# Second channel matmul as seven products of half blocks in place of eight, in a fused attention and MLP-mixer kernel

## The chip, the cores and the metric

The kernel runs on one core of a Trainium2 chip. The metric is the device time of one execution in microseconds (us): the median of 16 runs, 273.47 us before the change (273.07 to 275.13). Five engines work side by side, each through its own queue in order: TensorE (PE, with its weight loads as PEld), VectorE (DVE), ScalarE (ACT), GpSimd (POOL) and SyncE (SP, which here only issues transfers). They wait for each other through semaphores.

## The reference

Eight batches of 576 positions, 8 heads of 64, f32 in and out.

```python
q_p = phi(q, cos_w, sin_w)          # relu(q)*cos | relu(q)*sin, 128 features a head
k_p = phi(k, cos_w, sin_w)
kv  = einsum('bhsf,bhsd->bhfd', k_p, v);  z = k_p.sum(axis=2)
x   = (q_p @ kv) / (q_p . z + 1e-6)           # [B, 576, 512]
u   = x + (relu(x^T @ w_tok1) @ w_tok2)^T     # token matmuls, 576 -> 256 -> 576
out = u + relu(u @ w_ch1) @ w_ch2             # channel matmuls, 512 -> 1536 -> 512
```

The change is in the last line: `relu(u @ w_ch1)` is called h1, and `h1 @ w_ch2` is the second channel matmul.

## The kernel before, in words

The 576 rows of a batch are spread over 128 partitions so that four full row tiles of 128 (J=4) and half a tile are left; the half tiles of two batches make one row tile. So each batch has a block of 4 x 128 rows, and the eight half tiles make a further block of 4 x 128 rows, the *tail* (`u_tail`, `uT_tail`). A block is what the channel matmuls work on.

All work is issued in an order written by hand. Batches 0 and 1 and the beginning of 2 and 3 come from the list `PLAN`. From batch 2 on, `channel(...)` issues a block's channel matmuls, and between them, at numbered *slots*, the work of the following batches that `hooks_for` has put there. While batch p's block is in `channel`, attention and token matmuls of batch n=p+1 are done, the features and transposes of m=p+2, and the loads of p+3.

`channel` (L576) has 12 steps for the first matmul (index mi): four matmuls of 512 columns into a PSUM tile `c_ps` from pool psM (four buffers), then a relu to `h1[:, mi, :]` in bf16 on ScalarE or VectorE, as `evac` says (L672), then the slot's hooks. The second matmul follows: for each of four row tiles j, 12 matmuls of 512 columns accumulate in `o_ps` (L606), VectorE adds the result to `u` (L609), and after the second and fourth row tile SP stores two of them. Each j has two slots (12 to 19). In the tail (`fine=True`) the last row tile is done in two column halves (L598, L600), and each row tile is stored at once by SP and ScalarE's queue (`store_tail`, L624).

Names that the prediction uses: `kvm`/`kvo` (L367, L377: kv of all heads: 40 narrow matmuls, and its copy on ScalarE), `numf`/`numfo` (L420, L425: q features times kv on TensorE, then two small VectorE instructions and a multiplication to `x`), `mix`/`mixo` (L429, L436: first token matmul and relu to `B1`), `um`/`uo`/`ubc`/`utx` (L456 to L474: second token matmul; VectorE adds `x` to give `u`; GpSimd casts to bf16 `ub`; a transposing transfer writes `uT`, the operand of the next block's first matmul), `tm`/`to`/`tb` (L485 to L503: the same for the half tile), `feat` (L323: a q or k feature, ScalarE "A" or VectorE "D"), `turnx` (L353: transposing transfer of q features to `qpT`), `cast` (L334: v to bf16 on GpSimd, "P"). Pools psA (two buffers of two banks) and psM are PSUM; `one` and `two` are pools with one and two buffers. A tile that is allocated again in a pool waits until the readers of the buffer's earlier tile are done.

`hooks_for` (L640) puts kv in slot 0, `num_all` in 2 to 6, `mix` in 7 and 8, `u_all` in 10, 11 and 12, the casts in 3 to 7, q features in 9 to 13 (two a slot, ScalarE), k features in 13 to 17 (two a slot, VectorE), `turnx` in 12, 15 and 16.

Of the kernel before, what the change touches and what calls it, by code (L numbers as in the profile page):

```python
# [9 lines left out]
F32 = mybir.dt.float32  # L10
BF16 = mybir.dt.bfloat16
AF = mybir.ActivationFunctionType
ALU = mybir.AluOpType

WARM = 20
FIRST = "S"
PLAN = """
feat.0.k.4.2.0.D feat.0.q.0.2.0.A feat.0.q.2.2.1.A feat.0.q.3.2.1.A feat.0.q.4.2.1.D feat.0.q.3.2.0.A
# [40 lines left out]
def kernel(  # L59
# [11 lines left out]
    nc = tc.nc  # L71

    B, H, S, D = q.shape
    Dm = H * D
    _, D_tok = moe_w_tok1.shape
    _, D_ch = moe_w_ch1.shape
    P = 128
    J = S // P
    JA = J + 1
    R = J + JA  # L80
    NP = B // 2
    NCC = Dm // P
    NT = D_tok // P
    NCH = D_ch // P
    HH = H // 2
    VW = D + 2
# [44 lines left out]
    def heads(g):  # L131
        return slice(0, H) if g == 2 else slice(g * HH, (g + 1) * HH)
# [30 lines left out]
    par = const.tile([P, 1], F32, name="par")  # L163
# [36 lines left out]
    for i in range(2):  # L200
        t = const.tile([P, JA, H, VW], BF16, name=f"vbf{i}")
# [7 lines left out]
    w2r = const.tile([P, NT, S], BF16, name="w2r")  # L209
    wc1 = const.tile([P, NCC, D_ch], BF16, name="wc1")  # L210
    wc2 = const.tile([P, NCH, Dm], BF16, name="wc2")
# [44 lines left out]
    u_tail = const.tile([P, NP, Dm], F32, name="u_tail")  # L256
    uT_tail = const.tile([P, NP, NCC, P], BF16, name="uT_tail")
# [8 lines left out]
    def relu(eng, dst, src):  # L266
        if eng == "A":
            nc.scalar.activation(dst, src, AF.Relu)  # L268
        else:
            nc.vector.tensor_relu(dst, src)  # L270

    class Batch:
# [4 lines left out]
        def sb(self, name):  # L277
            if not hasattr(self, name):
                pool, shape, dt = {
                    "kp": (one, [P, JA, H, 2, D], BF16), "qp": (one, [P, JA, H, 2, D], BF16),  # L280
                    "qpT": (two, [P, JA * H, P], BF16), "kv": (two, [P, H, VW], BF16),
                    "x": (two, [P, JA, Dm], BF16), "B1": (two, [P, NT, Dm], BF16),
                    "u": (two, [P, J, Dm], F32), "ub": (one, [P, J, Dm], BF16),
                    "uT": (two, [P, J, NCC, P], BF16), "h1": (one, [P, NCH, 4 * P], BF16)}[name]
                setattr(self, name, pool.tile(shape, dt, name=name))
            return getattr(self, name)
# [248 lines left out]
        def o(self, j):  # L535
            nc.vector.tensor_add(self.u[:, j, :], self.ps.pop(("o", j)), self.u[:, j, :])
            if j % 2:
                for p_ in range(2):
                    nc.sync.dma_start(out=out_rows(self.b, p_, j - 1, 2), in_=self.u[p_::2, j - 1:j + 1, :])
# [36 lines left out]
    def channel(uT, u, store, by_slot, hooks, fine=False):  # L576
        h1 = one.tile([P, NCH, 4 * P], BF16, name="h1")
        slot = 0

        def step():  # L580
            nonlocal slot
            for f in hooks.get(slot, ()):
                f()
            slot += 1

        for mi in range(NCH):
            c_ps = psM.tile([P, 512], F32, name="c_ps", tag="psM")
            for ki in range(NCC):
                nc.tensor.matmul(c_ps, wc1[:, ki, mi * P:(mi + 1) * P], uT[:, :, ki, :],  # L589
                                 start=(ki == 0), stop=(ki == NCC - 1))  # L590
            relu(by_slot[mi], h1[:, mi, :], c_ps)
            step()
        for j in range(4):
            if fine and j == 3:
                for cs in (slice(0, Dm // 2), slice(Dm // 2, Dm)):
                    o_ps = psM.tile([P, Dm // 2], F32, name="o_ps", tag="psM")
                    for ki in range(NCH):
                        nc.tensor.matmul(o_ps, h1[:, ki, j * P:(j + 1) * P], wc2[:, ki, cs],  # L598
                                         start=(ki == 0), stop=(ki == NCH - 1))
                    nc.vector.tensor_add(u[:, j, cs], o_ps, u[:, j, cs])  # L600
                    store(j, u, cs)
                break
            o_ps = psM.tile([P, Dm], F32, name="o_ps", tag="psM")
            for half in range(2):
                for ki in range(half * NCH // 2, (half + 1) * NCH // 2):
                    nc.tensor.matmul(o_ps, h1[:, ki, j * P:(j + 1) * P], wc2[:, ki, :],  # L606
                                     start=(ki == 0), stop=(ki == NCH - 1))
                if half:
                    nc.vector.tensor_add(u[:, j, :], o_ps, u[:, j, :])  # L609
                    store(j, u)  # L610
                step()

    def out_rows(b, par, j, n):
        f = JA * par + j if j < J else J
        return out[b].rearrange("(m r) c -> m r c", r=R)[:, f:f + n, :]

    def store_batch(b):
        def store(j, u):
            if j % 2:
                for par in range(2):  # L620
                    nc.sync.dma_start(out=out_rows(b, par, j - 1, 2), in_=u[par::2, j - 1:j + 1, :])
        return store

    def store_tail(j, u, cs=slice(0, Dm)):  # L624
        for c, eng in ((0, nc.sync), (1, nc.scalar)):
            eng.dma_start(out=out_rows(2 * j + c, c, J, 1)[:, :, cs], in_=u[c::2, j:j + 1, cs])


    bt = [Batch(b) for b in range(B)]
    OPS = {"ld": ld, "ldp": ldp, "mkid": lambda: make_identity(nc, ident), "wt1": wt1, "wt2": wt2, "wu": wu, "wd": wd, "w2a": w2a}  # L630
    keep_warm(WARM)
    for word in PLAN.split():
        name, *a = word.split(".")
        a = [int(x) if x.isdigit() else x for x in a]
# [5 lines left out]
    def hooks_for(n, m, nxt):  # L640

        h = {}

        def at(slot, f, *a):
            h.setdefault(slot, []).append(lambda: f(*a))
        if nxt is not None:
            at(0, load, nxt, "k")
            at(0, load, nxt, "q")
            if nxt > 5:
                at(9, load, nxt, "v")  # L650
        if n is not None:
            at(0, n.kv_all)
            for j in range(JA):
                at(2 + j, n.num_all, j)
            for j in range(JA):
                at(7 + j // 3, n.mix, j, 2)
            at(8, n.mix_out)
            for g in range(3):
                at(10 + g, n.u_all, g)
        if m is not None:  # L660
            for j in range(JA):
                at(3 + j, m.cast, j, 1, 2, "P")
                at(9 + j, m.q_feature, j)
                at(13 + j, m.k_feature, j)
            at(12, m.turnx, 0, 2)
            at(15, m.turnx, 2, 2)
            at(16, m.turnx, 4, 1)
        if nxt == 5:
            at(16, load, nxt, "v")
        return h  # L670

    evac = ["A"] * 7 + ["D", "A", "D", "D", "D"]  # L672
    for p in range(2, B):
        s = bt[p]
        n = bt[p + 1] if p + 1 < B else None
        m = bt[p + 2] if p + 2 < B else None
        nxt = p + 3 if p + 3 < B else None
        channel(s.uT, s.u, store_batch(p), evac if n else ["A", "D"] * 6, hooks_for(n, m, nxt))
    channel(uT_tail, u_tail, store_tail, ["A", "D"] * 6, {}, fine=True)

    _ = tile, bass_utils

# [29 lines left out]
```

## Time and profile before

| what | value |
|---|---|
| median of 16 runs | 273.47 us (273.07 to 275.13) |
| profiled execution | 273.31 us, its span 271.5 us |
| granted TensorE clock | 1.00 |
| batches 2 to 6 (start of the first channel matmul) | 88.1, 115.7, 143.3, 170.9, 198.4 us |
| batch 7, tail, last matmul ends | 226.0, 246.7, 267.5 us |
| VectorE busy in those five batches | 19.71, 18.88, 19.45, 17.58, 14.30 us |
| ScalarE busy in them | 12.51, 12.51, 12.51, 12.51, 6.39 us |
| GpSimd: cast of v, of ub (512, 1024 elements) | 0.614, 1.04 us |
| VectorE: k feature, numfo multiplication, relu from PSUM | 0.48, 0.69, 0.69 us |
| ScalarE: relu, q feature, relu to B1 | 0.60, 0.71, 1.02 us |
| landing of a transposing transfer, ub to uT, qp to qpT (median) | 3.2, 4.4 us |

The page gives for each engine its busy time and the number of its instructions; the stages give the same for a stretch of the span; the groups give one line of code on one engine, its shapes, count, total and mean time in ns, and then the idle time before it and what ended it. The chain of work is followed back from the last instruction to whatever released it, so it names what set the end. A matmul's duration in the groups (0.38 us for 512 columns) is longer than the distance from one to the next, since they overlap; the chain shows the distance.

### The profile page before, as it was taken

Reading aid. Unit: us, or ns where it says so; the run is one execution under the profiler, and the core shown is the slowest. Engines: PE = TensorE matmul, PEld = TensorE weight load, DVE = VectorE, ACT = ScalarE, POOL = GpSimd, SP = SyncE. Lnnn points to the kernel's source line nnn. Section 1 sums busy time; section 2 is a strip of 40 time slices with the busy share of each in tenths; the row PEclk is TensorE's granted clock in tenths of the full one; section 3 lists DMA queues with packets and bytes.
Section 4 is the critical chain, followed back from the end, with each engine's and each line's share of the span. In section 5 each row is a group of like instructions: output and inputs, shape, how many; then the busy total and the mean of one; then the engine's idle time right before and its main releaser. Section 6 shows DMA issues by size and latency. Waiting matters only on the chain.

```text
span 271.5 us, 4868 instructions
## 1 busy us (share of the span) xinstructions
PE 262.8 (97%) x1941; PEld 137.8 (51%) x1941; DVE 172.3 (63%) x346; ACT 111.1 (41%) x176; POOL 47.1 (17%) x67
## 2 busy tenths in 40 slices
PE   6988999999999999999999999999999999999994
PEld 2875556455444644464445544554455444444443
DVE  6489788899872658845794679467837643423422
ACT  2885281475490548044904490439033102201300
POOL 2154070040051043003350036003000210000000
PEclk9999999999999999999999999999999999999999
DMA  6999999999999999999999978900970062012012
GB/s 197 359 232 154 277 248 227 367 226 230 377 233 210 333 380 295 230 164 338 360 203 255 327 223 193 226 0 19 218 193 2 1 172 80 0 57 98 2 69 86
DMA packets 79079, 53.37 MB, mean 197 GB/s; under 512 B 47824, under 2 KB 76496, under 8 KB 79056
## 3 DMA queue, kind: packets, MB, share of 16 engines
q1 hardware_dynamic: 74512, 48.77, 66.8%
q0 software_dynamic: 4144, 3.77, 9.0%
q10 hardware_dynamic: 400, 0.52, 0.5%
q8 instruction: 15, 0.25, 0.3%
q14 instruction: 8, 0.07, 0.1%
HBM read 35.85 MB, written 9.44 MB: 167 GB/s over the span
## 4 chain that ended last, share of the span: by engine, by line
PE 91%; DVE 4%; DMA 3%; issue 0%; DVEq 0%
PE c_ps L589 27%; PE o_ps L606 26%; PE o L524 8%; PE c L512 8%; PE b L433 6%; PE u L460 5%; PE kv L361 4%; PE nf L390 3%; DMA kt<-in_k_dram 3%; PE ut L488 1%; PE tr L345 1%; DVE kp L332 1%; PE o_ps L598 1%; PE nm L390 1%; PE uT L450 1%; DVE x L413 1%
## 5 line engine op out<-in xcount | busy, mean ns | idle before, releaser
L268 ACT ACTIVATE h<-c_ps 128x512 bf16<-128x512 f32 x52 | 31.0, 597 | 107.6 <-PE c_ps L589 64.2
L606 PE MATMUL o_ps<-wc,h 128*128 128x512 bf16 x324 | 71.9, 379 | 0.0
L589 PE MATMUL c_ps<-uT,wc 128*128 128x512 bf16 x288 | 70.4, 379 | 0.0
L606 PEld LDWEIGHTS <-h 128*128 128x128 bf16 x324 | 31.7, 98 | 38.2
L589 PEld LDWEIGHTS <-wc 128*128 128x128 bf16 x336 | 30.8, 98 | 32.6
L270 DVE TENSOR_SCALAR h<-c_ps 128x512 bf16<-128x512 f32 x32 | 22.0, 688 | 28.4 <-PE c_ps L589 28.4
L264 POOL CAST ub<-u 128x1024 bf16<-128x1024 f32 x14 | 15.1, 1080 | 89.3 <-DVE u L465 45.8
L264 POOL CAST vbf<-vt 128x512 bf16<-128x512 f32 (+3 forms) x28 | 18.8, 708 | 64.9 <-DMA vt<-in_v_dram 51.5
L330 ACT ACTIVATE qp<-qt,cos_t 128x512 bf16<-128x512 f32 x33 | 23.1, 712 | 13.6 <-DMA qt<-in_q_dram 12.8
L609 DVE TENSOR_TENSOR u<-o_ps,u 128x512 f32<-128x512 f32 x24 | 16.6, 690 | 18.8 <-PE o_ps L606 18.6
L512 PE MATMUL c<-uT,wc 128*128 128x512 bf16 x96 | 22.7, 379 | 0.0
L524 PE MATMUL o<-wc,h 128*128 128x512 bf16 x96 | 22.0, 379 | 0.0
L413 DVE TENSOR_TENSOR x<-nf,den 128x512 bf16<-128x512 f32 x30 | 20.7, 691 | 1.0
L330 ACT ACTIVATE qp<-qt,sin_t 128x512 bf16<-128x512 f32 x30 | 21.1, 712 | 0.0
L465 DVE TENSOR_TENSOR u<-u,x 128x1024 f32<-128x1024 f32 x16 | 19.3, 1219 | 2.2 <-PE u L460 2.2
L332 DVE TENSOR_SCALAR kp<-kt,cos_t 128x512 bf16<-128x512 f32 x30 | 17.4, 584 | 4.9 <-DMA kt<-in_k_dram 4.9
L433 PE MATMUL b<-x,w 128*128 128x512 bf16 (+1 forms) x90 | 20.3, 355 | 0.0
L390 PEld LDWEIGHTS <-qpT 128*128 128x128 bf16 x320 | 15.3, 98 | 9.6 <-DVE x L413 1.5
L332 DVE TENSOR_SCALAR kp<-kt,sin_t 128x512 bf16<-128x512 f32 x31 | 17.5, 571 | 0.8 <-DMA kt<-in_k_dram 0.8
L460 PE MATMUL u<-B,w 128*128 128x512 bf16 x64 | 16.1, 379 | 0.0
L409 DVE TENSOR_SCALAR den<-nf 128x8 f32<-128x8 f32 x30 | 5.0, 166 | 15.9 <-PE nf L390 15.9
L524 PEld LDWEIGHTS <-h 128*128 128x128 bf16 x96 | 9.0, 97 | 10.2
(92 smaller groups left out, 250.4 us busy)
## 6 DMA issues: line engine op xcount, KB each, us to landing
out_dram<-u SPq DMA_DIRECT2D x32, 256.0 KB, 2.8
qt<-in_q_dram SPq DMA_DIRECT2D x8, 640.0 KB, 8.1
kt<-in_k_dram SPq DMA_DIRECT2D x8, 640.0 KB, 8.1
qt<-in_q_dram SPq DMA_DIRECT2D x8, 512.0 KB, 7.0
kt<-in_k_dram SPq DMA_DIRECT2D x8, 512.0 KB, 7.0
vt<-in_v_dram SPq DMA_DIRECT2D x6, 640.0 KB, 8.2
vt<-in_v_dram SPq DMA_DIRECT2D x6, 512.0 KB, 7.2
wc<-in_moe_w_ch_dram POOLq DMA_DIRECT2D x4, 384.0 KB, 7.7
```

The costliest lines, as they stand in the source:

```text
L264: (nc.scalar.copy if eng == "A" else ENG[eng].tensor_copy)(dst, src)
L268: nc.scalar.activation(dst, src, AF.Relu)
L330: nc.scalar.activation(dst, src, AF.Relu, scale=tab)
L332: ENG[eng].tensor_scalar(dst, src, scalar1=tab, scalar2=0.0, op0=ALU.mult, op1=ALU.max)
L390: nc.tensor.matmul(nm[:, hh * (D + 1):(hh + 1) * (D + 1)], self.qpT[:, j * H + h, :], self.kv[:, h, :D + 1], start=(not eps or hh == 0), s ...
L413: nc.vector.tensor_mul(dst, nmv[:, :, :, :D], den_b)
L433: nc.tensor.matmul(b1[:, mi], w1[:, col(self.c, j), mi * P:(mi + 1) * P], self.x[:, j, cs], start=(j == 0 and (g == 2 or mi == 0)), stop=( ...
L460: nc.tensor.matmul(ps[:, jj], w2[:, ki, 1 + 2 * g + jj, :], self.B1[:, ki, :], start=(ki == 0), stop=(ki == NT - 1))
L512: nc.tensor.matmul(ps, wc1[:, ki, mi * P:(mi + 1) * P], self.uT[:, :, ki, :], start=(ki == 0), stop=(ki == NCC - 1))
L524: nc.tensor.matmul(self.ps["o", j], self.h1[:, ki, j * P:(j + 1) * P], wc2[:, ki, :], start=(ki == 0), stop=(ki == NCH - 1))
L589: nc.tensor.matmul(c_ps, wc1[:, ki, mi * P:(mi + 1) * P], uT[:, :, ki, :], start=(ki == 0), stop=(ki == NCC - 1))
L606: nc.tensor.matmul(o_ps, h1[:, ki, j * P:(j + 1) * P], wc2[:, ki, :], start=(ki == 0), stop=(ki == NCH - 1))
```

## The change

The second matmul of a block is h1 (rows x 1536) times w_ch2 (1536 x 512). Both are cut into 2 x 2 quarters: h1 into a11, a12 (first two row tiles; contraction chunks 0 to 5 and 6 to 11), a21, a22 (last two), w_ch2 into q00, q01, q10, q11. Eight products of quarters are replaced by seven, with sums of quarters as operands and sums of products as results (a Winograd form of Strassen's scheme). For batches 2 to 7 (p from QUADS=2) and the tail, `channel7` takes the place of `channel`. Sums of the weights (`t1` in the place of q01, `t2`, `t3`, `t4`) are made once, in batch 2's slots 0 and 8. A product has 2 row tiles x 6 chunks = 12 matmuls with 256 columns. The sums of h1 (`s1`, `s2`, `a21` in place) are made by VectorE in bf16; the sums of products by VectorE, and GpSimd for two on `u22`, after ScalarE has copied three products from PSUM to f32 in SBUF (`va`, `vb`, `vc`). Slots 12 to 18 follow the products, and all stores of a block stand behind the last. Other moves: in these batches q features go to slots 1 to 6 and 9 to 12, k features to 7, 8 and 13 to 17, of which six of ten go to ScalarE; two relus go from VectorE to ScalarE (`evac7`); `u_all(2)` goes to slot 18; `qpT` and `x` have one buffer instead of two.

```diff
-                    "qpT": (two, [P, JA * H, P], BF16), "kv": (two, [P, H, VW], BF16),
-                    "x": (two, [P, JA, Dm], BF16), "B1": (two, [P, NT, Dm], BF16),
+                    "qpT": (one, [P, JA * H, P], BF16), "kv": (two, [P, H, VW], BF16),
+                    "x": (one, [P, JA, Dm], BF16), "B1": (two, [P, NT, Dm], BF16),
...
+    t1 = quad(0, 1)
+    def quad_weights():
+        return [lambda: nc.vector.tensor_sub(t3, quad(1, 1), quad(0, 1)),
+                lambda: nc.vector.tensor_sub(t1, quad(0, 1), quad(0, 0)),
+                lambda: nc.gpsimd.tensor_sub(t2, quad(1, 1), t1),
+                lambda: nc.vector.tensor_sub(t4, quad(1, 0), t2)]
...
+        a11, a12, a21, a22 = tok(0, 0), tok(1, 0), tok(0, 1), tok(1, 1)
...
+        for mi in range(NCH):
...
+            relu(by_slot[mi], h1[:, mi, :], c_ps)
+            if mi == NCH - 2:
+                s_part(s1, nc.vector.tensor_add, a21, a22, 0)
+                s_part(s2, nc.vector.tensor_sub, s1, a11, 0)
+            if mi == NCH - 1:
+                s_part(s1, nc.vector.tensor_add, a21, a22, 1)
+                s_part(s2, nc.vector.tensor_sub, s1, a11, 1)
+            step()
+        Dk = bank()
...
+            A = bank()
+            product(A, a11, quad(0, 0), True)
+            nc.scalar.copy(va, A)
+        nc.vector.tensor_sub(a21, a11, a21)
+        step()
+        product(Dk, a22, t4, True)
+        nc.scalar.copy(vb, Dk)
+        nc.gpsimd.tensor_sub(u22, u22, vb)
+        step()
+        Bk = bank()
+        product(Bk, s2, t2, True)
+        nc.vector.tensor_add(va, Bk, va)
+        nc.vector.tensor_sub(s2, a12, s2)
+        step()
+        C = bank()
+        product(C, s1, t1, True)
+        nc.scalar.copy(vc, C)
+        nc.vector.tensor_add(u12, u12, va)
+        nc.gpsimd.tensor_add(u22, u22, vc)
+        step()
+        product(Dk, a21, t3, False)
+        nc.vector.tensor_add(vb, Dk, va)
+        step()
...
+        product(C, s2, quad(1, 1), False)
+        if fine:
+            nc.vector.tensor_add(u2, u2, wide)
+            store(2, u, 2)
+            nc.vector.tensor_add(u12, C, u12)
+            store(0, u, 2, slice(D2, Dm))
+            step()
+            for jj in range(2):
+                product(A, a12, quad(1, 0), False, (jj,))
+                nc.vector.tensor_add(u11[:, jj], A[jj], u11[:, jj])
+            store(0, u, 2, slice(0, D2))
+        else:
+            nc.vector.tensor_add(u12, C, u12)
+            step()
+            product(A, a12, quad(1, 0), False)
+            nc.vector.tensor_add(u11, A, u11)
+            store(0, u, 2)
+            nc.vector.tensor_add(u2, u2, wide)
+            store(2, u, 2)
...
+            for i, slot in enumerate((1, 2, 3, 4, 5, 6, 9, 10, 11, 12)):
+                at(slot, m.feat, "q", i // 2, 2, i % 2, "A")
+            for i, slot in enumerate((7, 7, 8, 8, 13, 14, 15, 16, 17, 17)):
+                at(slot, m.feat, "k", i // 2, 2, i % 2, "D" if i < 4 else "A")
...
+    evac7 = ["A"] * 7 + ["D", "A", "A", "D", "A"]
+    evac2 = ["A"] * 4 + ["D", "A"] * 4
```

`s_part(..., n)` does chunks 0 to 3 (n=0) or 4 and 5 (n=1) of a quarter; `wide` reads `vb` twice, for both column halves; A, Dk, Bk and C are psM tiles, two of which take a second product later. In the prediction the products are counted in the order issued: A, D (the tile Dk), B, C, and then again into D, C and A.

More of the change, by code (lines that the diff above doesn't have):

```diff
@@ L15 @@
 WARM = 20
+QUADS = 2
 FIRST = "S"
@@ L611, in channel, with quad @@
                 step()
+    K2, D2 = NCH // 2, Dm // 2
+    t2, t3, t4 = (const.tile([P, K2, D2], BF16, name=f"t{i}") for i in (2, 3, 4))
+    def quad(a, b):
+        return wc2[:, a * K2:(a + 1) * K2, b * D2:(b + 1) * D2]
+    t1 = quad(0, 1)
[4 more added lines that the diff above has]
+                lambda: nc.vector.tensor_sub(t4, quad(1, 0), t2)]
@@ new lines, in channel7, with step, tok, s_part @@
+    def channel7(uT, u, store, by_slot, hooks, fine=False):
+        h1 = one.tile([P, NCH, 4 * P], BF16, name="h1")
+        slot = 0
+        def step():
+            nonlocal slot
+            for f in hooks.get(slot, ()):
+                f()
+            slot += 1
+        def tok(a, b):
+            return h1[:, a * K2:(a + 1) * K2, b * 2 * P:(b + 1) * 2 * P]
+        a11, a12, a21, a22 = tok(0, 0), tok(1, 0), tok(0, 1), tok(1, 1)
+        s1 = one.tile([P, K2, 2 * P], BF16, name="s1")
+        s2 = one.tile([P, K2, 2 * P], BF16, name="s2")
+        va = w2r.rearrange("p n s -> p (n s)").bitcast(F32)[:, :2 * D2].rearrange("p (a b) -> p a b", a=2)
+        vb = one.tile([P, 2, D2], F32, name="vb")
+        vc = one.tile([P, 2, D2], F32, name="vc")
+        u11, u12 = u[:, 0:2, :D2], u[:, 0:2, D2:]
+        u21, u22 = u[:, 2:4, :D2], u[:, 2:4, D2:]
+        def s_part(dst, f, a, b, n):
+            ks = (slice(0, 4), slice(4, K2))[n]
+            f(dst[:, ks], a[:, ks], b[:, ks])
+        def product(ps, a, b, first, jjs=(0, 1)):
+            for jj in jjs:
+                for ki in range(K2):
+                    nc.tensor.matmul(ps[jj] if isinstance(ps, list) else ps[:, jj], a[:, ki, jj * P:(jj + 1) * P], b[:, ki],
+                                     start=(first and ki == 0 and (jj == 0 or isinstance(ps, list))), stop=ki == K2 - 1,
+                                     skip_group_check=True)
+        def bank():
+            return psM.tile([P, 2, D2], F32, name="m_ps", tag="psM")
+        for mi in range(NCH):
+            c_ps = psM.tile([P, 512], F32, name="c_ps", tag="psM")
+            for ki in range(NCC):
+                nc.tensor.matmul(c_ps, wc1[:, ki, mi * P:(mi + 1) * P], uT[:, :, ki, :],
+                                 start=(ki == 0), stop=(ki == NCC - 1))
+            relu(by_slot[mi], h1[:, mi, :], c_ps)
[8 more added lines that the diff above has]
+        if fine:
+            A = [bank()[:, 0], psA.tile([P, D2], F32, name="m2_ps", tag="psA")]
+            for jj in range(2):
+                product(A, a11, quad(0, 0), True, (jj,))
+                nc.scalar.copy(va[:, jj], A[jj])
+        else:
[22 more added lines that the diff above has]
+        step()
+        wide = bass.AP(tensor=vb.tensor, offset=vb.offset, ap=[vb.ap[0], [D2, 2], [0, 2], [1, D2]])
+        u2 = u[:, 2:4, :].rearrange("p j (a d) -> p j a d", a=2)
+        product(C, s2, quad(1, 1), False)
+        if fine:
+            nc.vector.tensor_add(u2, u2, wide)
[3 more added lines that the diff above has]
+            step()
+            for jj in range(2):
+                product(A, a12, quad(1, 0), False, (jj,))
+                nc.vector.tensor_add(u11[:, jj], A[jj], u11[:, jj])
+            store(0, u, 2, slice(0, D2))
+        else:
+            nc.vector.tensor_add(u12, C, u12)
[5 more added lines that the diff above has]
+            store(2, u, 2)
+        step()
+        step()
@@ L617, in store_batch, with store, store_tail @@
     def store_batch(b):
[L618 to L621, printed above, removed]
-        return store
-    def store_tail(j, u, cs=slice(0, Dm)):
+        def store(j, u, n=1, cs=None):
+            if n == 1 and j % 2 == 0:
+                return
+            j -= j % 2
+            for par in range(2):
+                nc.sync.dma_start(out=out_rows(b, par, j, 2), in_=u[par::2, j:j + 2, :])
+        return store
+    def store_tail(j, u, n=1, cs=slice(0, Dm)):
+        rows = out.rearrange("b (m r) c -> m r b c", r=R)[:, J]
         for c, eng in ((0, nc.sync), (1, nc.scalar)):
-            eng.dma_start(out=out_rows(2 * j + c, c, J, 1)[:, :, cs], in_=u[c::2, j:j + 1, cs])
+            eng.dma_start(out=rows[:, 2 * j + c:2 * (j + n):2, cs], in_=u[c::2, j:j + n, cs])
     bt = [Batch(b) for b in range(B)]
@@ L670, in hooks_for, with hooks7, at @@
         return h
+    def hooks7(n, m, nxt, quads):
+        h = {}
+        def at(slot, f, *a):
+            h.setdefault(slot, []).append(lambda: f(*a))
+        if nxt is not None:
+            at(0, load, nxt, "k")
+            at(0, load, nxt, "q")
+            at(16 if nxt == 5 else 9, load, nxt, "v")
+        if n is not None:
+            at(0, n.kv_all)
+            for j in range(JA):
+                at(2 + j, n.num_all, j)
+            for j in range(JA):
+                at(7 + j // 3, n.mix, j, 2)
+            at(8, n.mix_out)
+            at(10, n.u_all, 0)
+            at(11, n.u_all, 1)
+            at(18, n.u_all, 2)
+        if m is not None:
+            for j in range(JA):
+                at(3 + j, m.cast, j, 1, 2, "P")
+            for i, slot in enumerate((1, 2, 3, 4, 5, 6, 9, 10, 11, 12)):
+                at(slot, m.feat, "q", i // 2, 2, i % 2, "A")
+            for i, slot in enumerate((7, 7, 8, 8, 13, 14, 15, 16, 17, 17)):
+                at(slot, m.feat, "k", i // 2, 2, i % 2, "D" if i < 4 else "A")
+            at(12, m.turnx, 0, 2)
+            at(14, m.turnx, 2, 2)
+            at(15, m.turnx, 4, 1)
+        if quads:
+            for f, slot in zip(quad_weights(), (0, 0, 0, 8)):
+                at(slot, f)
+        return h
     evac = ["A"] * 7 + ["D", "A", "D", "D", "D"]
+    evac7 = ["A"] * 7 + ["D", "A", "A", "D", "A"]
+    evac2 = ["A"] * 4 + ["D", "A"] * 4
     for p in range(2, B):
@@ L677 @@
         nxt = p + 3 if p + 3 < B else None
-        channel(s.uT, s.u, store_batch(p), evac if n else ["A", "D"] * 6, hooks_for(n, m, nxt))
-    channel(uT_tail, u_tail, store_tail, ["A", "D"] * 6, {}, fine=True)
+        if p < QUADS:
+            channel(s.uT, s.u, store_batch(p), evac, hooks_for(n, m, nxt))
+        else:
+            channel7(s.uT, s.u, store_batch(p), evac7 if n else evac2, hooks7(n, m, nxt, p == QUADS))
+    channel7(uT_tail, u_tail, store_tail, evac2, {}, fine=True)
     _ = tile, bass_utils
```

## The prediction

> **What bounds the kernel now.** I read the busy totals first, then the busy time by stage, then the chain that ended last in order of time. Totals (page, part 1), and two of the stages, one batch each (us, then PE, PEld, DVE, ACT, POOL busy, each with its count):
>
> ```profile
> PE 262.8 (97%) x1941; PEld 137.8 (51%) x1941; DVE 172.3 (63%) x346; ACT 111.1 (41%) x176; POOL 47.1 (17%) x67
> ...
> 115.70:143.30 27.60, 27.60 (x197) 13.88 (x196) 18.88 (x37) 12.51 (x20) 8.62 (x12) 1.00 1.11 270
> 226.00:246.70 20.70, 20.70 (x98) 9.41 (x96) 6.91 (x10) 3.58 (x6) 0.00 (x0) 1.00 0.13 51
> ```
>
> In a batch's 27.6 us TensorE is busy for 27.6, at a granted clock of 1.00, while the next engine, VectorE, has about 8 us free. So work taken from TensorE comes off the time, as long as no other engine becomes late. The chain of work, batch 3 and the end:
>
> ```profile
> 131.60 0.86 PE u L460 x4
> 132.47 1.29 PE o_ps L606 x6
> 133.76 0.43 PE ut L488 x2
> 134.19 9.06 PE o_ps L606 x42
> 143.26 0.86 PE c_ps L589 x4
> ...
> 257.09 7.77 PE o_ps L606 x36
> 264.86 2.63 PE o_ps L598 x24
> 267.52 0.42 DVE u_tail L600
> ```
>
> From 88 to 267.5 us the chain is TensorE alone. It gives both prices: a 512-column matmul takes 7.77/36 = 0.216, a 256-column one 2.63/24 = 0.1096, its own 98 ns weight load hidden.
>
> **What leaves and enters TensorE.** One second matmul is 48 x 0.216 = 10.36 (1.29 + 9.06). It becomes seven products of 12 matmuls with 256 columns: 84 x 0.1096 = 9.21, or 1.315 a product. Saved: 1.15 in each of batches 2 to 7 (the blocks from p=2 on), 6.9 in all. The tail costs 7.77 + 2.63 = 10.40 now: 1.19 saved. Together **8.1 us**. First matmul, attention and token matmuls are the same.
>
> A rule of the Trainium skill speaks against this: "TensorE: Matmul & The Clock Gate", section Back-to-back issue gap, gives sustained streams of weight load and matmul 131 ns at N=512 and 81 at N=128. By that, 48 matmuls are 6.3 us and 84 of width 256 (by a straight line between, an estimate, 98 ns) 8.2: the change would lose 1.9 a time. Here 512 columns take 216 ns and 256 take 110, so I use the rows.
>
> **What VectorE gets.** Per batch it loses six k features (6 x 0.48) and two relus (2 x 0.69), and four 0.69 adds are replaced. It gains four 512-element f32 adds (0.69: `va`, `vb`, and u12 twice), the u11 add (0.69), the wide u2 add (1.22, as L465), and bf16 adds within SBUF: `s1`, `s2` (1024 and 512 elements each), `a21` and the second `s2` (1536). The trace has no such add. Fast bound: 0.52 ns an element, as the bf16 copies at L264 (1024 in 682 ns, 512 in 417), so 0.42 / 0.68 / 0.95. Slow bound: 1.03 ns an element, as the f32 adds:
>
> ```profile
> L497 DVE TENSOR_TENSOR u_tail<-u_tail,x 128x512 f32<-128x512 f32 x4 | 2.8, 692 | 0.1
> ...
> L465 DVE TENSOR_TENSOR u<-u,x 128x1024 f32<-128x1024 f32 x16 | 19.3, 1219 | 2.2 <-PE u L460 2.2
> ```
>
> that is 0.69 / 1.22 / 1.75. All operands are bf16 with unit step; "VectorE: DVE Perf Modes", The perf-mode tier table, gives tensor_tensor twice its f32 rate in that case; no row here shows it. I take the fast bound. The six ops then cost 4.1 us (slow: 7.3).
>
> Whether they hide is decided in queue order. Let t=0 be the end of first-matmul tile 10. TensorE then does um(0), tile 11, um(1) (0.86 each), A and D: the third product, which needs `s2`, can start at 2.6 + 2.6 = 5.2. VectorE's queue: relu 0.69, s1 0.68, s2 0.68, uo(0) 1.22, s1 0.42, s2 0.42: 4.1, so 1.1 spare. Then uo(1) 1.22 and a21 0.95: 6.3, needed by the fifth product at 7.85. `va` waits for the third product (6.5), then 0.69, then s2 0.95: 8.2, needed by the sixth at 9.2: 1.0 spare. No stall. `u11`, `u2` and the tail-row add run into the next batch's first 2.2 us or so; its first VectorE work (numfo) is due after about 4.1.
>
> **ScalarE.** Sixteen features (11.4), ten relus (6.0), kv and B (1.6), three PSUM copies (1.8 by the relu's 0.6): 20.8 of some 26.4 us. Tight only in slots 1 to 6, where q features now stand: relu + feature 1.31 against TensorE's 0.86 + 0.26 = 1.12, so it falls 1.1 behind; the four psM buffers allow about three tiles, 3.4. From slot 7 it has over 2 us with one tile. The first q feature also waits until the transposes of the preceding q features (now one `qpT` buffer, one `qp`) have landed: the last is issued some 0.5 us into the batch, lands in 4.4 (part 6), near 5; the relus behind it would hold TensorE only past 6 to 6.5. The vb copy is due at 7.85 and ready near 5.9. No charge.
>
> **GpSimd and the queues.** Two f32 adds a batch. Nearest row: a one-input 512-element cast, 0.61; two inputs by "GPSIMD Engine Reference", Elementwise — side-by-side cycle accounting, take about twice VectorE's time, an estimate of 1.4; I take 1.4, due only at u2's add. The same page, Key points, warns of shared SBUF interfaces when VectorE has two SBUF inputs. This trace shows sharing between casts and k features:
>
> ```profile
> 138.72 0.48 DVE L332 TENSOR_SCALAR kp<-kt,cos_t 128x512 bf16<-128x512 f32 x1
> 139.12 0.83 DVE L332 TENSOR_SCALAR kp<-kt,sin_t 128x512 bf16<-128x512 f32 x1
> ...
> 138.78 3.70 POOL L264 CAST vbf<-vt 128x512 bf16<-128x512 f32 x5 [3.94 <-DMA vt<-in_v_dram]
> ```
>
> 0.48 becomes 0.83, and five casts take 3.70 instead of 2.84. Now ub's casts meet the second s1/s2 pair and a21, and the first u22 add the last s2: +0.35 each, two on the third product's path (spare 1.1), one on the sixth's (spare 1.0). Still covered; without the warning these spares stand whole.
>
> SP issues as many transfers per batch; turnx of q moves ahead of the stores, stores behind the seventh product. What gets closer is `uT`: uo(1), ubc (1.04), utx (landing 3.2) end at 5.3 to 5.7 + 1.1 + 3.3 = 10; the next batch needs it after 5.2 + 5 x 1.315 + 0.43 = 12.2. Only in batch 3 a v load is in flight, and a landing took 6.3: 0 to 1.1 late. I charge 0.3. The weight differences (three 1536-element VectorE subtractions, one on GpSimd, once) lie at batch 2's start, where VectorE is idle some 3 us.
>
> **End.** Now the last add ends 0.45 after TensorE. Then the wide add (waiting for GpSimd near 7.3 after the first matmul's end) 1.22, u12 0.69, u11 twice 0.42 end about 0.65 after: +0.2. All four tail rows are stored within 1.3 us instead of one every 2.6, and the last store has 128 KB per queue (2.0 to 2.3 us to landing now) not 64 (1.8 to 2.1): +0.2, and 0 to 0.8 for queueing: I take 0.3. End: +0.7.
>
> **Sum.** The profiled execution took 273.31 (span 271.5 plus 1.8), 0.16 under the median 273.47. 273.31 - 8.1 + 0.7 + 0.3 = 266.2; with a part of the 0.16, **266.3**.
>
> **Rivals.** (1) *Cover holds*, above: 265.2 to 267.6 (the end at 0.4 to 1.5, the uT wait at 0 to 1.1, the matmul at 0.1085 to 0.1096). 62%.
> (2) *Partly late*: port sharing or ScalarE's lag uses up spares of about 1 us, each of the five full batches stalls 0.3 to 0.8: 266.3 + 1.5 to 4 = 267.8 to 270.3. For: the spares are shorter than two or three +0.35. Against: they need overlap at the worst places. 23%.
> (3) *Slower: VectorE's queue becomes the bound between tile 10 and the sixth product.* At the slow bound its durations add to 5.7 at the third product's operand (due 5.2), 8.7 at a21, and 8.7 + 0.69 + 1.75 = 11.2 at the last s2, due at 9.2: 2.0 per full batch, 10 in five: 275.9. Overlapped starts (the trace has about 0.09 between an instruction's start and its forerunner's end) would make it 1.2, 272; GpSimd sharing adds back. It decides from 7.4/5 = 1.5 us a batch. For: no row shows the fast rate. Against: the bf16 copies do run at the fast rate, and VectorE's total stays under the period. 9%.
> (4) *Narrow matmuls don't keep 110 ns*: with weight loads binding at 123, seven products cost what eight did: 273.3 to 274, with the end. Against: 24 in a row at L598 and the 256-column ones at L433. 6%.
>
> The range 265.2 to 269.6 takes (1) and most of (2). A measurement tells apart about 0.2%, 0.55 us: faster 0.87, same 0.03, slower 0.10.
>
> **What will show it.** Right: product matmuls 12 in 1.31, TensorE without gaps in batches, period 26.4 against 27.6, the 1536-element VectorE adds near 0.95. Wrong: these at 1.75; idle TensorE time ahead of the third, fifth or sixth product put to VectorE; ahead of a batch's first matmul put to the uT transfer; c_ps waiting for a relu on ScalarE in slots 5 to 7; the last store over 1.5 us later after TensorE's end.

## The result, and the profile after

The changed kernel takes 269.42 us (median of 8 runs, 268.59 to 270.35) against 273.56 before (45 runs): a ratio of 0.9848, 95% interval 0.9836 to 0.9861. It is faster by 4.1 us; the forecast said 7. The time lies only 0.2 us inside the upper end of the range (269.6); a ninth execution of 271.96 us is on record and isn't among these eight, and with it the median would be 269.66, just outside. The profiled execution took 270.35 us, 0.9 above the median, its span 268.2.

First the totals (page, part 1) and the two stages, batch 3 and batch 7 (us, then PE, PEld, DVE, ACT, POOL busy):

```profile
PE 256.0 (95%) x2181; PEld 161.2 (60%) x2181; DVE 200.8 (75%) x367; ACT 143.5 (53%) x236; POOL 76.5 (29%) x82
```

```profile
114.74:141.99 27.25, 26.55 (x233) 17.29 (x231) 22.41 (x39) 18.36 (x31) 11.51 (x13) 1.00 1.04 281
223.23:242.76 19.53, 19.53 (x133) 12.93 (x132) 11.94 (x18) 6.53 (x11) 3.14 (x3) 1.00 0.17 61
```

Batch 7, with no other work between its matmuls, went from 20.70 to 19.53: the 1.2 us that were promised. Batch 3 went only from 27.60 to 27.25, and for the first time TensorE isn't busy all through it. Batches 2 to 6 take 26.58, 27.25, 27.44, 27.40 and 26.40 (they were 27.6 each), the tail from its start to its last matmul 19.5 instead of 20.8. The chain of work says what the gaps of batches 3 and 4 are:

```profile
116.88 0.88 PE c_ps L667 x4
...
117.78 0.18 ACT h L269
117.96 3.13 DMA qpT<-qp
...
121.33 0.72 ACT qp L331
122.05 0.49 ACT h L269
...
135.38 1.68 POOL ub L265
137.06 0.03 POOL u L691
137.09 4.76 DMA uT<-ub
...
141.99 1.02 PE c_ps L667 x4
...
159.83 9.17 PE m_ps L657 x84
```

The last of these lines is the price of seven products, 9.17 us, or 0.1092 a matmul. The others are two waits: a q feature (L331) on ScalarE that waits for a transposing transfer, with the relu (L269) that TensorE needs standing behind it; and batch 4's first matmul that waits for `uT`. The same wait of ScalarE stands at 145.75 in batch 4 and 171.49 in batch 5.

The new VectorE and GpSimd work (groups, shapes kept apart; the last columns are busy us, mean ns):

```profile
L701 DVE TENSOR_TENSOR u<-u,w2r 128x512 f32<-128x512 f32 x6 | 9.5, 1575 | 0.0
L702 POOL TENSOR_TENSOR u<-u,vc 128x512 f32<-128x512 f32 x6 | 9.3, 1548 | 1.9 <-ACT vc L700 1.5
...
L687 DVE TENSOR_TENSOR h<-h 128x1536 bf16<-128x1536 bf16 x7 | 6.6, 945 | 0.0
L652 DVE TENSOR_TENSOR s<-s,h 128x512 bf16<-128x512 bf16 x7 | 6.6, 936 | 0.2
...
L652 DVE TENSOR_TENSOR s<-h 128x1024 bf16<-128x1024 bf16 x7 | 4.8, 681 | 0.0
...
L652 DVE TENSOR_TENSOR s<-h 128x512 bf16<-128x512 bf16 x7 | 2.9, 416 | 0.0
```

1536 elements take 945 ns, 1024 take 681 and 512 take 416: the forecast's fast bound. But an operation of the same 512 elements (the second part of `s2`) takes 936 in the mean, and the f32 addition of L701 takes 1575 where 690 was expected. These two meet GpSimd: in the five full batches, where a GpSimd cast or addition runs beside them, they take 1.14 and 1.76 us; in batch 7 0.42 and 0.69, with next to nothing of GpSimd beside them.

Last, the end. TensorE's last matmul ends at 253.12 + 9.17 = 262.3, and 5.9 us later the span ends; before it was 4.0. In order of time, and then the landing of the tail's stores (KB each, median us from issue to landing):

```profile
260.57 1.23 DVE L711 TENSOR_TENSOR u_tail<-u_tail,vb 128x1024 f32<-128x1024 f32 x1
...
261.71 0.68 DVE L713 TENSOR_TENSOR u_tail<-m_ps,u_tail 128x512 f32<-128x512 f32 x1
261.82 2.17 SPq L747 DMA_DIRECT2D out_dram<-u_tail  x3
261.83 2.34 ACTq L747 DMA_DIRECT2D out_dram<-u_tail  x3
262.31 0.74 DVE L718 TENSOR_TENSOR u_tail<-m_ps,u_tail 128x256 f32<-128x256 f32 x2
```

```profile
out_dram<-u_tail SPq DMA_DIRECT2D x1, 256.0 KB, 2.5
out_dram<-u_tail ACTq DMA_DIRECT2D x1, 256.0 KB, 3.2
out_dram<-u_tail SPq DMA_DIRECT2D x2, 128.0 KB, 2.9
out_dram<-u_tail ACTq DMA_DIRECT2D x2, 128.0 KB, 3.1
```

The last addition ends at 263.05, 0.75 after TensorE (0.45 before). Three stores per queue are issued back to back, some 0.7 us each, so the last one's issue is over at 264.0 to 264.2; it lands about 3 us after its issue began, where the last stores of before took 2. So the last landing is 4.3 us after TensorE's end and was 2.6 before. Of these 1.7 us, 0.7 is the later issue and 1.0 the longer landing.

### The profile page after: what moved, and what is told of

Same layout as the page of the kernel before. It is cut to its first block, busy times and chain, and to the rows that moved or that the text cites. A ratio compares the mean times of both kernels' runs of the same rounds, so it can differ in the third digit from the quotient of the medians.

```text
span 268.2 us, 5496 instructions
## 1 busy us (share of the span) xinstructions
PE 256.0 (95%) x2181; PEld 161.2 (60%) x2181; DVE 200.8 (75%) x367; ACT 143.5 (53%) x236; POOL 76.5 (29%) x82
## 4 chain that ended last, share of the span: by engine, by line
PE 79%; DMA 9%; DVE 5%; issue 2%; ACT 2%; POOL 1%; DVEq 0%; ACTq 0%; POOLq 0%
PE c_ps L667 23%; PE m_ps L657 20%; PE o L525 8%; PE c L513 8%; PE b L434 6%; PE u L461 5%; DMA qpT<-qp 4%; PE kv L362 4%; DMA kt<-in_k_dram 3%; DMA uT<-ub 2%; PE nf L391 2%; DVE kp L333 1%; PE tr L346 1%; PE ut L489 1%; POOL ub L265 1%
## 5 line engine op out<-in xcount | busy, mean ns | idle before, releaser
L269 ACT ACTIVATE h<-c_ps 128x512 bf16<-128x512 f32 x66 | 39.4, 597 | 48.5 <-PE c_ps L667 31.2
L265 POOL CAST ub<-u 128x1024 bf16<-128x1024 f32 x14 | 18.8, 1344 | 78.7 <-DVE u L466 72.5
L657 PEld LDWEIGHTS <-h 128*128 128x128 bf16 x336 | 32.9, 98 | 5.3
L331 ACT ACTIVATE qp<-qt,cos_t 128x512 bf16<-128x512 f32 x33 | 23.4, 722 | 23.5 <-DMA qt<-in_q_dram 11.6
L271 DVE TENSOR_SCALAR h<-c_ps 128x512 bf16<-128x512 f32 x18 | 12.4, 688 | 20.7 <-PE c_ps L667 20.7
L657 PEld LDWEIGHTS <-s 128*128 128x128 bf16 x252 | 24.5, 98 | 3.2 <-DVE s L696 0.3
L331 ACT ACTIVATE qp<-qt,sin_t 128x512 bf16<-128x512 f32 x30 | 21.5, 724 | 0.0
L657 PE MATMUL m_ps<-wc,s 128*128 128x256 bf16 x168 | 20.6, 273 | 0.0
L657 PE MATMUL m_ps<-wc,h 128*128 128x256 bf16 x168 | 20.6, 273 | 0.0
L657 PE MATMUL m_ps<-t,h 128*128 128x256 bf16 x168 | 20.6, 273 | 0.0
L331 ACT ACTIVATE kp<-kt,sin_t 128x512 bf16<-128x512 f32 x21 | 14.8, 714 | 4.0 <-DMA kt<-in_k_dram 2.3
L333 DVE TENSOR_SCALAR kp<-kt,cos_t 128x512 bf16<-128x512 f32 x18 | 10.4, 580 | 7.1 <-DMA kt<-in_k_dram 7.1
```

The lines of the kernel that those rows point to most:

```text
L265: (nc.scalar.copy if eng == "A" else ENG[eng].tensor_copy)(dst, src)
L331: nc.scalar.activation(dst, src, AF.Relu, scale=tab)
L657: nc.tensor.matmul(ps[jj] if isinstance(ps, list) else ps[:, jj], a[:, ki, jj * P:(jj + 1) * P], b[:, ki], start=(first and ki == 0 and (j ...
```

## The experiments

Theory W: ScalarE's first q feature of a batch waits for all three transposes of the batch before, since its tile `qp` is allocated anew; the relus behind it stop TensorE. Theory E: the end grew because the whole tail is added up and stored at once. Rivals: VectorE's queue and its sharing with GpSimd (V), ScalarE's load in slots 1 to 6 (S), and for the end, other stores.

In the table, "batches 2 to 5" is the time in the profile from batch 2's first matmul to batch 6's (105.6 when TensorE never waits), "relu" is how long TensorE stood idle there for a relu on ScalarE. A wait costs somewhat more than its idle time: in e9 batches 4 and 5 lose 0.7 and 0.4 us to waits of 0.4 and 0.2.

| kernel | median us (runs) | ratio to before, 95% | start of batch 2 | batches 2 to 5 | relu |
|---|---|---|---|---|---|
| changed kernel | 269.42 (8) | 0.9836 to 0.9861 | 88.0 | 108.7 | 1.4 |
| e1_split_qp | 269.45 (6) | 0.9808 to 0.9859 | 90.0 | 106.9 | 0 |
| e2_tail_old | 268.29 (4) | 0.9775 to 0.9814 | 88.2 | 108.5 | 0.9 |
| e3_moves_only | 273.41 (12) | 0.9979 to 1.0006 | 89.3 | 110.3, no wait | 0 |
| e4_last_alone | 268.26 (4) | 0.9784 to 0.9820 | 88.6 | 107.6 | 0.4 |
| e5_shared_qp | 269.19 (5) | 0.9809 to 0.9858 | 88.9 | 106.6 | 0 |
| e6_shared_old | 266.62 (4) | 0.9722 to 0.9766 | 88.0 | 106.0 | 0 |
| e7_no_pool_u22 | 266.90 (4) | 0.9739 to 0.9835 | 87.9 | 106.3 | 0 |
| e8_vload16 | 266.87 (4) | 0.9727 to 0.9768 | 87.9 | 105.9 | 0 |
| e9_after_again | 269.50 (6) | 0.9831 to 0.9880 | 88.3 | 107.0 | 0.6 |
| e10_shared_again | 268.59 (5) | 0.9801 to 0.9847 | 87.8 | 106.6 | 0 |
| e11_both_again | 267.53 (4) | 0.9759 to 0.9803 | 87.9 | 107.3 | 0 |
| e12_tail_reorder | 268.55 (6) | 0.9788 to 0.9847 | 88.4 | 107.1 | 0 |

**e1: q features in three tiles.**

```diff
-  "qp": (one, [P, JA, H, 2, D], BF16),
+  "qp0": (one, [P, 2, H, 2, D], BF16), "qp1": (one, [P, 2, H, 2, D], BF16), "qp2": (one, [P, 1, H, 2, D], BF16),
```

> The changed kernel, but the q features lie in three tiles (row tiles 0 and 1, 2 and 3, 4) instead of one, so that a q feature waits only for the transpose that reads its own tile, not for all three of the batch before. Theory W (in batches 3, 4 and 5 ScalarE's first q feature waits for the last of these transposes, the relus queue behind it and TensorE runs out of free psM buffers; 27.25, 27.44 and 27.40 us instead of 26.4): these three become about 26.4 to 26.6, and the median falls from 269.42 by 2 to 2.8, to about 267. Rival V (the lost time in these batches comes from VectorE's longer queue and its sharing with GpSimd, and the wait only shows where it surfaces): the periods stay at 27.2 or more, the median within 0.5 of 269.4.

The stages did what W says, 26.6, 26.8 and 26.5 us instead of 27.25 to 27.44; the median did nothing. In its profile batch 2 begins 2.0 us later. The split holds for the first batches too and loosens what they wait for, so this run alone settles nothing.

**e2: the old tail.**

```diff
-    channel7(uT_tail, u_tail, store_tail, evac2, {}, fine=True)
+    channel(uT_tail, u_tail, lambda j, u, cs=slice(0, Dm): store_tail(j, u, 1, cs), ["A", "D"] * 6,
+            {0: [lambda: nc.vector.tensor_add(t1, t1, quad(0, 0))]}, fine=True)
```

> The changed kernel, but the tail's channel matmuls as before (eight products' work, row tile by row tile, each stored when it is done); one VectorE addition at the tail's start makes the weight quarter q01 again from t1 and q00. Theory E (the end after the last matmul grew from 4.0 to 5.9 us because all four row tiles of the tail are added up and stored in the last 2 us): TensorE ends 1.2 us later, the end behind it is back at 4.0, so the time falls by 0.5 to 0.8, to 268.8. Rival (the end is longer for another reason, such as stores of the batch before that are still under way): the time rises by 1.2 to 270.6.

268.29: 1.1 us less although TensorE does 1.2 us more, so by the medians the end gained 2.3. The chain's last lines and the stores of this kernel:

```profile
260.91 2.63 PE o_ps L599 x24
263.54 0.02 issue
263.56 0.42 DVE u_tail L601
```

```profile
out_dram<-u_tail SPq DMA_DIRECT2D x2, 64.0 KB, 1.8
out_dram<-u_tail ACTq DMA_DIRECT2D x2, 64.0 KB, 2.1
```

From 263.54 to the end of the span at 267.1 is 3.6 us. Theory E holds. Some 0.35 of it lies outside the span: the changed kernel takes 2.1 us besides its span (270.35 - 268.2), this one 1.8, as before. What sets that part isn't shown: e7 has the old tail and takes 2.1, e12 has seven products in its tail and takes 1.9.

**e3: the moves alone.**

```diff
-            channel7(s.uT, s.u, store_batch(p), evac7 if n else evac2, hooks7(n, m, nxt, p == QUADS))
+            channel(s.uT, s.u, store_batch(p), evac7 if n else evac2, hooks7(n, m, nxt, False))
...
-    channel7(uT_tail, u_tail, store_tail, evac2, {}, fine=True)
+    channel(uT_tail, u_tail, lambda j, u, cs=slice(0, Dm): store_tail(j, u, 1, cs), ["A", "D"] * 6, {}, fine=True)
```

> The moves without the products: every block, the tail too, has the second matmul of before (48 matmuls of 512 columns), but q and k features stand in the slots of the changed kernel, six of ten k features and two more relus are on ScalarE, u_all(2) is in slot 18, and qpT and x have one buffer. Theory W: the transposes are issued earlier against the end of the batch, since no s1/s2 work delays u and eight products lie behind them; they land before ScalarE's wait holds TensorE, and the time is that of before within 0.3 (273.5). Rival S (ScalarE with 1.31 us of work a slot in slots 1 to 6 is itself what makes TensorE wait): batches 2 to 5 lose about 1 us each here too, 276 to 277.5.

273.41, the time of before, and every batch 27.58 with no wait of TensorE. ScalarE in batch 3 of this kernel, in order of time:

```profile
120.09 0.60 ACT L269 ACTIVATE h<-c_ps 128x512 bf16<-128x512 f32 x1 [0.27 <-PE c_ps L590]
120.59 0.71 ACT L331 ACTIVATE qp<-qt,cos_t 128x512 bf16<-128x512 f32 x1
121.20 0.59 ACT L269 ACTIVATE h<-c_ps 128x512 bf16<-128x512 f32 x1
121.68 0.72 ACT L331 ACTIVATE qp<-qt,sin_t 128x512 bf16<-128x512 f32 x1
```

Relu and feature alternate without a gap and cost TensorE nothing: rival S falls. The moves by themselves are free; the trouble needs moves and products together. Here the last transpose lands 3.2, 3.2 and 4.2 us into batches 3 to 5; in the changed kernel it is 6.5, 6.9 and 7.0.

**e4: the last store alone** (two of the tail's three stores are left out, so its output lacks these rows).

```diff
             nc.vector.tensor_add(u2, u2, wide)
-            store(2, u, 2)
             nc.vector.tensor_add(u12, C, u12)
-            store(0, u, 2, slice(D2, Dm))
```

> The changed kernel without two of the tail's stores: the two row tiles 2 and 3 and the right half of row tiles 0 and 1 of the tail are not written; the last store (left half of row tiles 0 and 1) is. Theory E as a burst (the last store is slow because 0.75 MB of stores go ahead of it within 1.3 us): its landing falls from 3.0 to 2.0-2.3 us, it is issued about 0.4 earlier, and the time falls by about 1.2. Rival (the last store is slow by its own size and shape, 128 KB per queue in pieces of 1 KB): landing stays near 3.0, time within 0.5 of 269.4.

The same 128 KB per queue now land in

```profile
out_dram<-u_tail SPq DMA_DIRECT2D x1, 128.0 KB, 2.2
out_dram<-u_tail ACTq DMA_DIRECT2D x1, 128.0 KB, 2.5
```

instead of 2.9 and 3.1, and the time is 1.2 us lower, as the burst says. So the store's own size and shape aren't what made it slow.

**e5: one q feature tile for batches 3 to 7, the list untouched.**

```diff
         def sb(self, name):
+            if name == "qp" and self.b >= 4:
+                self.qp = bt[3].sb("qp")
```

> The changed kernel; batches 4 to 7 write their q features into batch 3's tile instead of a newly allocated one, so that a feature waits only for the transpose that reads the same row tiles, and the hand-written list for the first batches stays as it is (splitting the tile for all batches had reached its aim in batches 3 to 5, 79.9 us for the three against 82.1, but lost 2.0 us ahead of batch 2). Theory W: batches 3, 4 and 5 fall to 26.4 to 26.8, batch 2 still begins at 88.2, and the median is 267 to 267.5. Rival (the gain there was only the other side of the loss ahead, since transfers had moved as a whole): 269 to 269.6 again.

Batches 3 to 5 took 26.4, 26.6 and 26.8, together 2.3 less than in the changed kernel's first profile, although the last transposes land as late as there, 5.3, 7.1 and 7.2 us into these batches: late landings without the wait on ScalarE cost TensorE nothing. But the median was only 0.2 lower: a miss for W's size. Batch 2 began at 88.9 in this profile, though nothing was changed ahead of it.

**e6: both repairs (e5 and e2).**

> Both repairs: the shared q feature tile, and the tail as before. If W and E are two independent losses, 269.4 - 2.2 - 1.1 = 266.1. If one hides the other, 267 or more.

266.62, ratio 0.9744 (0.9722 to 0.9766), 0.5 from the sum. ScalarE in batch 3 of this kernel, beside the same place in the changed kernel:

```profile
117.93 0.60 ACT L269 ACTIVATE h<-c_ps 128x512 bf16<-128x512 f32 x1 [0.27 <-PE c_ps L669]
118.43 0.71 ACT L333 ACTIVATE qp<-qt,cos_t 128x512 bf16<-128x512 f32 x1
119.04 0.59 ACT L269 ACTIVATE h<-c_ps 128x512 bf16<-128x512 f32 x1
```

```profile
117.78 0.60 ACT L269 ACTIVATE h<-c_ps 128x512 bf16<-128x512 f32 x1 [0.27 <-PE c_ps L667]
121.33 0.72 ACT L331 ACTIVATE qp<-qt,cos_t 128x512 bf16<-128x512 f32 x1 [2.95 <-DMA qpT<-qp]
121.95 0.58 ACT L269 ACTIVATE h<-c_ps 128x512 bf16<-128x512 f32 x1
```

The feature follows its relu at once in the first; in the second ScalarE stood still for 2.95 us.

**e7: both repairs, without GpSimd's work on u22** (the lower right quarter then lacks two products).

```diff
-        nc.gpsimd.tensor_sub(u22, u22, vb)
...
-        nc.gpsimd.tensor_add(u22, u22, vc)
```

> Both repairs, and GpSimd's two additions on u22 in each block left out (the lower right quarter of the result lacks these two products). If the sharing of SBUF between VectorE and GpSimd costs time (second s2 1.17 instead of 0.95, u12 + va 1.76 instead of 0.69), these fall back to 0.95 and 0.69 and each of the five full batches gets up to 0.2 us shorter than with both repairs alone, up to 1 us in all. If the spare times hold, no difference beyond 0.2 us.

Of the two durations only one moved. Groups of this kernel, where L697 is the second s2 and L702 the addition of `va` to u12:

```profile
L697 DVE TENSOR_TENSOR s<-h,s 128x1536 bf16<-128x1536 bf16 x6 | 6.8, 1132 | 0.0
L654 DVE TENSOR_TENSOR s<-s,h 128x512 bf16<-128x512 bf16 x6 | 6.1, 1022 | 0.2
...
L702 DVE TENSOR_TENSOR u<-u,w2r 128x512 f32<-128x512 f32 x6 | 4.1, 679 | 0.0
```

u12's addition fell from 1575 to 679 ns, so GpSimd's two-input additions had made it slow; the s2 operations stay slow, 1132 and 1022, beside the casts of ub that remain. The time didn't move (266.90 against 266.62 and 267.53). The slowing of u12 is real and large, and here it lies in spare time: rival V as a cause of the lost time falls as far as u22's additions go. The sharing with the casts wasn't taken away, so its part in making `u` and `ub` late stays argued. In e5, e6 and e8 all of the sharing is there, and batches 3 to 5 are at 26.4 to 26.8: by itself, without the late transfers, it costs TensorE next to nothing.

**e8: both repairs, v loads behind the uT transfers.**

```diff
-            at(16 if nxt == 5 else 9, load, nxt, "v")
+            at(16, load, nxt, "v")
```

> Both repairs, and the v loads of batches 6 and 7 issued in slot 16 instead of 9, that is behind the transfers that write uT. If batch 4's first matmul waits for uT because of the v load in flight (landing 4.8 us instead of 3.3), batch 3 becomes 26.4, 0.3 to 0.4 us shorter than with both repairs alone. If it is because u and ub are late, no difference.

In batch 3 the two uT transfers land in 3.3 and 3.4 us (3.9 and 6.1 in e6), so a v load in flight does delay them. But batch 3 was 26.40 in both profiles: in e6 even 6.1 us were in time. The time is the same, 266.87. In e11, with a landing of 7.3, TensorE then waited 0.9.

**e9 to e12, on one chip.**

> The changed kernel, once more, beside the next two on the same chip: the shared q feature tile alone brought the median down by only 0.2 us although its profile showed batches 3 to 5 shorter by 2.3, its batch 2 beginning 0.9 later. If that start of batch 2 differs by chance from execution to execution, the changed kernel's median here is 269 to 269.8 and its start in this profile need not be 88.0. Theory W: batches 3 to 5 take 27.2 to 27.5 each again, whatever the start.

> The shared q feature tile alone, once more. Theory W with a start that varies by chance: batches 3 to 5 together 79.3 to 79.9 us, and the median 1 to 2.3 below the changed kernel's of this call. Rival (what these batches gain is lost elsewhere for a reason): within 0.5 of the changed kernel's again.

> Both repairs once more: 266.3 to 266.9; the step from the shared tile alone is the tail's, 1.1 as it was from the changed kernel, if the two losses are independent.

The changed kernel came again at 269.50, in this profile with batches of 26.8, 26.4, 27.1 and 26.8. TensorE's waits in it:

```profile
PE c_ps L667 <- ACT h L269: 0.6, 2, 0.4
...
PE c_ps L667 <- DMA uT<-ub: 0.5, 1, 0.5
```

So W's wait is smaller here than in the first profile (1.4), and once didn't stop TensorE at all. The shared tile gave 268.59 (0.9 less), both repairs 267.53 (1.1 less again, the tail's share as in e2). Over all profiles the relu's wait is in each of the four (changed kernel, e2, e4, e9) that allocate `qp` anew and have the products in the batches (0.4 to 1.4 us), and in none of the eight with a repair. Within the four it goes with the landing of the last transpose: where that came 5.2 to 6.1 us into the batch, TensorE didn't wait (4 cases of batches 3 to 5); where it came at 6.4 to 7.0, TensorE waited 0.2 to 0.6 (8 cases). That is the mechanism shown. Its price is less certain: in medians 0 to 0.9 us with the new tail, 0.8 to 1.7 with the old, less than the 2.3 between the first profiles, of which the changed kernel's was a slow one of its eight. Set against the kernel of before, run beside each, the new tail has ratios of 0.9848 and 0.9855 without the repair and 0.9833, 0.9834 and 0.9824 with it: about 0.6 us, with intervals that overlap. Why e1 and e5 kept so little stays open. The start of batch 2 differs between the profiles, by up to 1.5 us where the code ahead of it is the same, and is a part of the spread.

**e12: the seventh product third in the tail.**

```diff
+        if fine:
+            for jj in range(2):
+                product(A, a12, quad(1, 0), False, (jj,))
+                nc.vector.tensor_add(u11[:, jj], A[jj], u11[:, jj])
+            store(0, u, 2, slice(0, D2))
...
-            nc.vector.tensor_add(u2, u2, wide)
-            store(2, u, 2)
+            nc.vector.tensor_add(u21, u21, vb)
+            store(2, u, 2, slice(0, D2))
+            nc.gpsimd.tensor_add(u22, u22, vb)
             nc.vector.tensor_add(u12, C, u12)
             store(0, u, 2, slice(D2, Dm))
-            for jj in range(2):
-                product(A, a12, quad(1, 0), False, (jj,))
-                nc.vector.tensor_add(u11[:, jj], A[jj], u11[:, jj])
-            store(0, u, 2, slice(0, D2))
+            store(2, u, 2, slice(D2, Dm))
```

> The shared q feature tile, and the tail with seven products in another order: the seventh (a12 times q10) is issued third, so that the left half of row tiles 0 and 1 is stored while four products are still to come; of row tiles 2 and 3 VectorE adds the left half and GpSimd the right half, each stored by itself. Theory E: TensorE ends 1.2 us earlier than with the old tail, the end behind it is between the 4.0 of the old tail and the 5.9 of the new, about 5.2, so the time equals that of both repairs within 0.3 (266.6). If what counts is only how much is stored after TensorE's end (768 of 1024 KB still is within 1 us), the end stays near 5.9 and the time is 0.7 above it.

268.55, the end 5.7 us after TensorE (5.9 in e9), equal to e10 and 1.0 above both repairs. Storing a quarter early isn't enough, as the rival says: GpSimd's last addition took 1.70 and ended 1.3 after TensorE, and three stores per queue still stood behind each other. The fastest version on record is both repairs, 266.6 to 267.5.

## Why the prediction was right, and where it was off

Direction and range held, the range with 0.2 us to spare; the likeliest case (266.3) did not. The figure is that of the case "partly late", in part by luck: not each of the five full batches stalled (batch 6 never did, and batch 3 not always), and about half of what was missing came from the end. By its steps:

- *What leaves TensorE*: 8.1 forecast. Measured 1.18 in batch 6, 1.19 in batch 7, 1.22 in the tail, so 7 x 1.19 = 8.3 without waits. Right: 84 matmuls took 9.17 us, so the rows were right against the rule of the Trainium skill that the prediction set beside them, which would have made the change a loss.
- *What VectorE gets*: the fast bound is measured (416, 681, 945 ns): 0.52 ns an element as forecast, half of the 1.03 of the f32 additions. Rival (3), slower, is out.
- *Sharing with GpSimd*: "+0.35 each" was too small: the second s2 of 512 elements takes 1.14 at most instead of 0.42 (+0.7), the last s2 1.17 (+0.22), u12's addition 1.76 (+1.07), GpSimd's additions 1.97 and 1.60 in the batches instead of 1.4. The spare times still held, but for 0.2 us once, ahead of batch 2's sixth product.
- *ScalarE*: the step that failed. "the last is issued some 0.5 us into the batch, lands in 4.4 (part 6), near 5 ... No charge." In batches 3, 4 and 5 of the changed kernel it was issued 3.4, 3.8 and 2.2 us into the batch and landed at 6.5, 6.9 and 7.0. The limit of 6 to 6.5 was right, so the wait turned into a stall. What was mis-sized is SyncE's queue ahead of it. In batches 2 to 3 of the changed kernel:

```profile
107.50 4.41 SPq L473 DMA_TRANSPOSE uT<-ub  x2
112.01 7.21 SPq L355 DMA_TRANSPOSE qpT<-qp  x3
```

  The first line took 2.98 before. The issues themselves did not get longer (1.27 and 1.23 us, as before): the second one waited for ub's second cast. It came 3.9 us before batch 3's start, where it had come 8.2 before. This is because `u` stands behind the new VectorE work and because of the sharing: the second s2 part takes 0.7 longer, ub's second cast 1.70 instead of 1.04. Then the three transposes of q features are issued without a gap in 7.2 us, the middle one alone in 3.6 to 3.9 (2.6 to 2.9 before). Since SP works in order, all of this adds up in front of the last transpose's landing. In the profile of before it was already issued up to 2.1 us into the batch.
- *uT*: 0.3 charged, in batch 3 only. The waits were 0.3 to 1.4 us in all, at the end of batch 2, of batch 3, or of both.
- *End*: +0.7 forecast, measured +1.9 in the span and +0.35 outside. The additions were about right (+0.3 for 0.2); the "0 to 0.8 for queueing: I take 0.3" was the term that was too small: three issues behind each other and a landing a full us longer.

The sum for the profile of e9, whose execution (269.06) is nearest the median: span before 271.5 - 8.3 + 1.9 (end) + 1.4 (lost in batches 2 to 5) + 0.4 (later start) = 266.9, as measured, and 0.35 more outside it. So of the 3.1 us that the forecast was low, the end with the part outside the span is about 1.5, the waits about 1.1, the rest start and chance.

## What to carry to other kernels

When work on a saturated engine is cut, add up the in-order queue of transfers (issue times, not only landings) as carefully as the engines: here each batch became shorter, and the same transposes became late against the next. In this kernel a tile that was allocated anew made its first writer wait for all readers of the old one (2.95 us in batch 3); writing into the same tile let each part wait for its own reader, and the relu's wait was gone. A rearrangement that completes all outputs at the end is worth less in the last block, where nothing hides the stores: there the version with less arithmetic lost 1.1 us.

## What the runs showed that was not expected

Operations of GpSimd and VectorE that both work within SBUF slowed each other by nearly the whole time that they overlapped, and the one that began second bore it. In batch 3, in order of time, first VectorE and then GpSimd:

```profile
135.22 0.94 DVE L687 TENSOR_TENSOR h<-h 128x1536 bf16<-128x1536 bf16 x1
...
137.79 1.76 DVE L701 TENSOR_TENSOR u<-u,w2r 128x512 f32<-128x512 f32 x1
```

```profile
135.36 1.70 POOL L265 CAST ub<-u 128x1024 bf16<-128x1024 f32 x1 [1.47 <-DVE u L466]
137.03 1.97 POOL L691 TENSOR_TENSOR u<-u,vb 128x512 f32<-128x512 f32 x1
```

The a21 operation (L687) began before the second cast and kept its 0.94 (0.95 alone); the cast took 1.70 where it takes 1.04 alone. The u12 addition (L701) began beside a GpSimd addition that had 1.2 us to go, and took 1.1 more than alone. GpSimd's addition takes 1.27 alone, in the tail. It looks as if the two take turns; no run varied only the order, so this is a reading of the trace and not a rule. Only the slowing of u12 was tested by taking GpSimd's work away (e7).
